# Moving the products of keys with values further back in a written-out order

## The chip, the cores and the metric

The kernel runs on one core of one Trainium2 chip. The metric is the device time of one execution in microseconds (us). Beside it a hardware profile of one execution is read: its span runs from the first to the last instruction.

## The reference

The inputs are queries, keys and values of 8 batches, 8 heads, 576 tokens and 64 features, and two weight matrices. The first block is an attention without a matrix of tokens by tokens; the second is a Fourier mix with a two-layer perceptron behind it.

```python
q_s = softmax of q over the features of a head
k_s = softmax of k over the tokens
kv  = np.einsum('bhsd,bhse->bhde', k_s, v)
x   = np.einsum('bhsd,bhde->bhse', q_s, kv)      # then heads side by side: (8, 576, 512)
u   = x + real(fft(fft(x, axis=1), axis=2))
un  = (u - mean(u)) / np.sqrt(var(u) + 1e-06)
out = u + np.maximum(un @ w_ch1, 0.0) @ w_ch2    # w_ch1: 512 x 2048, w_ch2: 2048 x 512
```

Everything is float32.

## The kernel before

The work goes batch by batch. A layer of the perceptron for one group of tokens runs on TensorE while the attention and the Fourier mix of the next group are threaded into it. The product with `w_ch1` is called *up* and the product with `w_ch2` *down*. Both use Strassen's scheme with seven products; in `up` a job of seven products is done four times (j = 0 to 3), and each uses two chunks of weights of 896 KB (`big<-w1s`), read from memory four chunks ahead. The products land in three banks, `ba`, `bb` and `bc`, in the order ba, bb, bc, bb, ba, bb, bc. Each product has two halves of four matmul instructions in the profile, and lines L1304, L1305, L1341, L1345 and L1346 bring the results from the banks, add and clip them on VectorE and ScalarE.

The order of all instructions is written by hand. Each piece of work is a *step* with a time; all steps of all groups are sorted by their time, and that order is what each engine gets. One unit of these times stands for 0.87 us. They are no waits: an engine runs its instructions in this order and waits only for data and buffers. The two halves of a product of `up` have one unit each.

`attention_timed(b, start, end)` gives the steps of the attention of batch b, which run during the `up` of the group before. `start` is 0 for b = 2 and 3 and -7 for b = 4 to 7. (Batches 0 and 1 have orders of their own.) In it:

- `keys(b)`: the maximum of the keys over the tokens (L695), exponentials (L699), and for each of four pairs of heads, r = 0 to 3: `turn` (L708, a transposition on VectorE of the keys), `times` (L715, the product of keys with values on TensorE, five matmul instructions of two passes), `scale` (L721 to L725, division by the sums on VectorE into the tile `kvr`).
- `values_to(b, h)`: four loads (L648) of one half of the values into the one tile `vt`. Half 0 serves r = 0 and 1, half 1 serves r = 2 and 3. Half 1 is loaded into the same tile, so it waits for the products r = 0 and 1.
- `keys_to(b)`: four loads (L638) of the keys of batch b into the one tile `kb`. The turned keys of r = 1 to 3 lie in that tile too, so the loads for the next batch wait for the product r = 3. `ahead(b)` places them, in the `up` of the group before.
- `own_exp`, `own_times_kv`: four query tiles (loads L743, maximum L756 on VectorE, subtraction L761 on GpSimd, transposition L764 on VectorE, exponentials `qT` L774 on ScalarE, product with `kvr` L790 on TensorE). For even b there is a shared tile of queries as well (turned by L912).
- `t_times_kv(b)`: the product of the shared tile with `kvr` (L1004).

All loads and most stores are issued by SyncE, one after the other; an issue that must wait holds back those behind it. Among them are the stores of results: rows as they are (L1611), and mirrored rows by way of memory, first out (L1618) and then from memory to memory (L1620).

Of the kernel before, what the change touches and what calls it, by code (L numbers as in the profile page):

```python
# [118 lines left out]
def at(t, script):  # L119
    return [(t + dt, step) for dt, step in script]  # L120
# [17 lines left out]
class _Block:  # L138
# [108 lines left out]
    def loads_first(self, fetch):  # L247
# [45 lines left out]
        def second(r):  # L293
# [4 lines left out]
            load(t[:, 4, :], self.v[1, S - P:, cols])  # L298

        order = [lambda: nc.gpsimd.memset(v[0:64, 4, :], 0.0), table, *(lambda r=r: keys(r) for r in range(NR)), lambda: queries(0),  # L300
                 lambda: values(0), lambda: queries(1), shared, lambda: values(2), shared_firsts, self.tables,
                 *(lambda r=r: second(r) for r in range(NR)), *(lambda i=i: fetch(i) for i in range(11))]
# [176 lines left out]
    def attention_timed(self, b, start, end):  # L479

        tail = [("t", b)] if b % 2 == 0 else []
        own = [("q", b, c, u) for c, u in ((0, 0), (0, 1), (1, 1), (1, 0))]
        places, shared = [6, 13.5, 21.5, 27.2], start + 12
        if tail:
            places = [8.5, 14, 21.5, 27.2]
        if start == 0:
            places, shared = [13.5, 20.5, 24, 27.2], 7
        steps = at(start, self.keys(b))
        for it in tail:
            steps += at(shared, self.q_exp(it)) + at(shared + 8, self.t_turn(it))  # L490
            steps += at(22.4 if start < 0 else 35, self.t_fold(it))
        for t, it in zip(places, own):
            steps += at(t, self.own_exp(it)) + at(t + 15, self.own_times_kv(it))
        loads = [(t - 7, t + 7.6, self.own_load(it)) for t, it in zip(places, own)]
        loads += [(shared - 13, shared + 8.4, self.t_load(it)) for it in tail]
        loads.sort(key=lambda s: s[0])
        free = [-99] * 3
        for i, (t, end, load) in enumerate(loads):
            if i > 1:
                steps += at(max(t, free[-3]), load)  # L500
            free.append(end)
        return steps + at((33 if start < 0 else 39) if tail else max(22, start + 26), self.t_times_kv(b))

    def ahead(self, b):


        steps = at(24 if b > 2 else 20, self.keys_to(b))
        steps += at(35 if b > 2 else 22.5, self.values_to(b, 0))
        q = [self.own_load(("q", b, 0, u)) for u in range(2)]
        if b % 2 == 0:  # L510
            q = [self.t_load(("t", b)), q[0]]
        return steps + at(46.5, q[0]) + at(50, q[1])
# [170 lines left out]

        return [(0, copies), (0.3 + 0.15 * (4 // by), least)]

    def keys(self, b):


        nc, V, kb = self.nc, self.nc.vector, self.kb
        box = {}  # L690

        def top(r):
            if r == 0:
                box["m"] = self.small.tile([P, 4 * NR], F32, tag="km16", name="km16", bufs=2)
            V.reduce_max(box["m"][:, 4 * r:4 * r + 4], kb[:, r], axis=AX.X, negate=True)  # L695

        def exp(g):
            k = kb[:, g // 4, g % 4]
            nc.scalar.activation(k, k, ACT.Exp, bias=box["m"][:, g:g + 1])  # L699

        def turn(r):
            if r == 0:
                t = self.work.tile([P, KT, HD], F32, tag="Z", name="Z", bufs=1)
                t = t[:].rearrange("p k n -> p (k n)")[:, 0:NC * P]
            else:
                t = kb[:, r - 1].rearrange("p g s -> p (g s)")
            to = box["k", r] = t.rearrange("p (c n) -> p c n", n=P)
            V.transpose(to.rearrange("p c (g s) -> p c g s", s=Q), kb[:, r].rearrange("p g (c s) -> p c g s", s=Q))  # L708

        def times(r):  # L710
            pk, k = self.acc((P, P + 1)), box.pop(("k", r))
            box[r] = pk
            a = (P + 1) * (r % 2)
            for c in range(NC):
                nc.tensor.matmul(pk, lhsT=k[:, c, :], rhs=self.vt[:, c, a:a + P + 1], start=c == 0, stop=c == NC - 1)  # L715

        def scale(r):
            pk = box.pop(r)
            rec = self.small.tile([P, 1], F32, tag="krec", name="krec", bufs=4)
            at = P * (r % 2)  # L720
            V.tensor_scalar(out=rec[:], in0=pk[:, at:at + 1], scalar1=ATT_EPS, scalar2=None, op0=ALU.add)  # L721
            V.reciprocal(rec[:], rec[:])
            for h in range(2):
                s, cols = slice(64 * h, 64 * h + 64), slice(64 * h + 1 - r % 2, 64 * h + 65 - r % 2)
                V.tensor_scalar(out=self.kvr[b % 2][s, r, s], in0=pk[s, cols], scalar1=rec[s, 0:1], scalar2=None, op0=ALU.mult)  # L725

        steps = [(0.9 * r, lambda r=r: top(r)) for r in range(NR)]
        steps += at(3.6, self.across(lambda: box["m"], 2, 4 * NR)) + at(4.5, self.across(lambda: box["m"], 1, 4 * NR))
        steps += [(6 + g / 2, lambda g=g: exp(g)) for g in range(4 * NR)]
        for r in range(NR):  # L730
            for dt, f in ((8.3, turn), (10.8, times), (12.5, scale)):
                steps.append((dt + 2 * r + 6 * (r > 1 and f != turn), lambda f=f, r=r: f(r)))
        steps += at(13.5, self.values_to(b, 1))
        return steps

    def own_load(self, it):
# [1038 lines left out]
```

## Time and profile before

| | us |
|---|---|
| median of 3 runs | 1054.22 |
| lowest, highest | 1052.79, 1058.33 |
| the profiled execution | 1057.53 |
| its span | 1055.8 |

In the rows of the timeline, the first number is the start in us from the span's start and the second the time to the end of the last of the instructions merged in the row; in brackets stands the idle time of the engine ahead of it and what ended it. A row of TensorE with x10 and line L715 is one product of keys with values. "PE" is TensorE, "DVE" VectorE, "ACT" ScalarE, "POOL" GpSimd and "SPq" the issuing of SyncE. Matmuls overlap by a little, so what one costs is read from one start to the next.

| | busy, us | share of the span |
|---|---|---|
| TensorE | 1037.7 | 98% |
| VectorE | 722.6 | 68% |
| ScalarE | 456.1 | 43% |
| GpSimd | 406.0 | 38% |

### The profile page before, as it was taken

To read this page: it belongs to the slowest core of one execution; us is meant where nothing else is said; L and a number is where in the kernel's file an instruction comes from. 1 tells how busy PE (TensorE), PEld (TensorE's weight loads), DVE (VectorE), ACT (ScalarE), POOL (GpSimd) and SP (SyncE) were. 2 spreads that over 40 slices of the span, in tenths; PEclk is the share of its full clock that TensorE was granted. 3 is DMA by queue.
4 is the path that set the end of the run, shared out by engine and by line. 5 is a ranking of instruction groups with operands and counts; after the bars stand their busy time and mean duration, and the time that the engine had idled before them with its cause. 6 is when DMAs were issued, how large, how long until landed. Compare 5 with 4: busy or idle time off the path is not lost.

```text
span 1055.8 us, 16768 instructions
## 1 busy us (share of the span) xinstructions
PE 1037.7 (98%) x6178; PEld 899.8 (85%) x6178; DVE 722.6 (68%) x1410; ACT 456.1 (43%) x1141; POOL 406.0 (38%) x350
## 2 busy tenths in 40 slices
PE   8999999899999999999999999999999999999998
PEld 7844555788888899889998999989998998999898
DVE  6898888665566876767765777688657644674563
ACT  5674433672248316751476236821682132131210
POOL 3164320257415645465545643474446450000000
PEclk9999999999999999999999999999999999999999
DMA  9787598586998666855677467757644664576464
GB/s 269 240 281 258 164 257 273 167 251 197 300 308 242 206 217 243 230 190 210 251 236 220 179 239 238 206 201 260 212 170 162 229 243 165 206 259 221 173 222 147
DMA packets 114313, 236.01 MB, mean 224 GB/s; under 512 B 23272, under 2 KB 78696, under 8 KB 103608
## 3 DMA queue, kind: packets, MB, share of 16 engines
q1 hardware_dynamic: 113864, 234.42, 67.7%
q8 instruction: 49, 0.80, 0.3%
q14 instruction: 32, 0.26, 0.1%
q10 hardware_dynamic: 288, 0.26, 0.1%
q0 software_dynamic: 80, 0.26, 0.1%
HBM read 199.79 MB, written 39.06 MB: 226 GB/s over the span
## 4 chain that ended last, share of the span: by engine, by line
PE 78%; DVE 5%; ACT 4%; DMA 3%; issue 1%; SPq 0%; POOL 0%; DVEq 0%; ACTq 0%
PE bb L1334 14%; PE bb L1461 10%; PE ba L1334 10%; PE bc L1334 9%; PE bc L1461 7%; PE ba L1461 7%; PE bb L1431 5%; PE acc L715 3%; ACT qT L774 2%; PE bb L1550 2%; PE acc L790 2%; PE acc L1087 1%; PE acc L1090 1%; DMA vt<-in_v_dram 1%; PE bc L1550 1%; PE ba L1550 1%
## 5 line engine op out<-in xcount | busy, mean ns | idle before, releaser
L1334 PE MATMUL bb<-unT,big 128*128 128x256 f32 x768 | 183.1, 381 | 0.1
L1334 PEld LDWEIGHTS bb<-unT,big 128*128 128x128 f32 x768 | 144.7, 191 | 19.9 <-DVE u L1304 1.0
L1346 ACT ACTIVATE big<-big 128x512 f32<-128x512 f32 x96 | 60.3, 629 | 170.8 <-DVE big L1345 169.9
L1334 PE MATMUL ba<-unT,big 128*128 128x256 f32 x512 | 124.0, 379 | 0.2 <-ACT big L1341 0.2
L774 ACT ACTIVATE qT<-q 32x128 f32<-32x128 f32 x384 | 117.9, 307 | 12.1 <-DVE q L764 7.1
L1334 PE MATMUL bc<-unT,big 128*128 128x256 f32 x512 | 121.8, 380 | 0.5 <-DVE big L1345 0.5
L1304 DVE TENSOR_TENSOR u<-bb,s 128x512 f32<-128x512 f32 x66 | 45.4, 687 | 94.5 <-PE bb L1334 79.5
L1334 PEld LDWEIGHTS bc<-unT,big 128*128 128x128 f32 x512 | 96.1, 190 | 14.2 <-DVE big L1345 1.8
L1334 PEld LDWEIGHTS ba<-unT,big 128*128 128x128 f32 x512 | 94.8, 190 | 12.6 <-ACT big L1341 0.6
L1461 PE MATMUL bb<-big 128*128 128x128 f32 x848 | 105.1, 275 | 0.3 <-DVE u L1468 0.3
L1461 PEld LDWEIGHTS bb<-big 128*128 128x128 f32 x848 | 99.6, 192 | 0.5 <-DVE u L1468 0.4
L1411 POOL TENSOR_TENSOR x<-x,big 128x512 f32<-128x512 f32 x45 | 57.7, 1296 | 63.5 <-DVE big L1468 31.2
L1461 PE MATMUL ba<-big 128*128 128x128 f32 x640 | 79.6, 275 | 0.0
L1461 PEld LDWEIGHTS ba<-big 128*128 128x128 f32 x640 | 76.3, 192 | 1.2
L1407 DVE TENSOR_TENSOR big<-big 128x512 f32<-128x512 f32 x98 | 75.3, 806 | 0.0
L761 POOL TENSOR_TENSOR q<-q,qm 128x512 f32<-128x512 f32 x24 | 25.8, 1073 | 116.1 <-DVE qm L756 73.0
L1210 POOL TENSOR_TENSOR unT<-unT 128x512 f32<-128x512 f32 x8 | 14.1, 1769 | 124.6 <-DVE unT L1210 124.6
L1468 DVE TENSOR_TENSOR u<-bb,s 128x256 f32<-128x256 f32 x40 | 16.8, 420 | 64.8 <-PE bb L1461 61.5
L1431 PE MATMUL bb<-big 128*128 128x256 f32 x256 | 58.7, 381 | 0.0
L384 POOL TENSOR_TENSOR big<-big 128x512 f32<-128x512 f32 x24 | 30.4, 1268 | 71.0 <-ACT big L1346 71.0
L1345 DVE TENSOR_TENSOR big<-bc,u 128x512 f32<-128x512 f32 x64 | 44.0, 687 | 18.6 <-PE bc L1334 17.8
L1431 PEld LDWEIGHTS bb<-big 128*128 128x128 f32 x256 | 48.2, 190 | 8.0 <-DVE big L1345 1.1
(279 smaller groups left out, 2032.2 us busy)
## 6 DMA issues: line engine op xcount, KB each, us to landing
big<-w2d SPq DMA_DIRECT2D x67, 1024.0 KB
big<-w1s SPq DMA_DIRECT2D x64, 896.0 KB
big<-w2s SPq DMA_DIRECT2D x16, 1024.0 KB
big<-in_w_dram SPq DMA_DIRECT2D x21, 512.0 KB
w2d<-big SPq DMA_DIRECT2D x42, 256.0 KB
kb<-in_kT_dram SPq DMA_DIRECT2D x24, 320.0 KB
q<-in_q_dram SPq DMA_DIRECT2D x28, 256.0 KB
vt<-in_v_dram SPq DMA_DIRECT2D x36, 160.0 KB
```

Of the source, the lines that this page charges most:

```text
L384: e1.tensor_tensor(out=to(4), in0=at(2), in1=at(3), op=ALU.add)
L715: nc.tensor.matmul(pk, lhsT=k[:, c, :], rhs=self.vt[:, c, a:a + P + 1], start=c == 0, stop=c == NC - 1)
L774: nc.scalar.activation(to[t, i * Q:i * Q + Q], one, ACT.Exp)
L1304: plus = lambda t: V.tensor_tensor(out=temp(t), in0=box["bb"][:], in1=box["s1"][:], op=ALU.add)
L1334: nc.tensor.matmul(bank()[:, i, :], lhsT=w[:, WA_AT[m], k * P:(k + 1) * P], rhs=self.unT[g][:, B_AT[m], k, :], start=first and i == 0 and ...
L1345: steps = [(0, lambda: V.tensor_tensor(out=hp(i), in0=bank()[:], in1=u()[:], op=ALU.add)), (0.8, lambda: nc.scalar.activation(hp(i), hp(i) ...
L1346: (0.8, lambda: nc.scalar.activation(hp(i), hp(i), ACT.Relu))]
L1407: e.tensor_tensor(out=to(o), in0=to(x), in1=to(y), op=op)
L1411: E.tensor_tensor(out=x, in0=x, in1=tile(m), op=ALU.add)
L1431: nc.tensor.matmul(box[name][:, i, :], lhsT=h[p][:, A_AT[m], i * P:(i + 1) * P], rhs=self.stream[n][:, p, :], start=p == 0 and (m != 1 or ...
L1461: nc.tensor.matmul(box[place[n]][:, i, :], lhsT=own(m)(A_AT[n])[:, f, :], rhs=w[:, r // 2, r % 2 * P:r % 2 * P + P], start=first and f == ...
L1550: nc.tensor.matmul(bank()[:, i, :], lhsT=h[p][:, A_AT[m], i * P:(i + 1) * P], rhs=w[:, p, :], start=first and i == 0 and p == 0, stop=p == ...
```

## The change

Only times of steps are changed. For all batches from 2 to 7, the products and scalings of r = 0 to 3 stand 1.5 units later, and so does the loading of the second half of the values. For b = 2 and 3 (start = 0), r = 2 and 3 stand another 2 units later, 3.5 in all. The loads of keys for b = 3 and 4 stand 3 units later (27 in place of 24), and the product of the shared tile's part for b = 3 follows (29 in place of 26; for b = 5 and 7 the larger of 22 and that is 22 in both). Nothing is computed differently, and no tile or buffer is added.

```diff
-        steps = at(start, self.keys(b))
+        steps = at(start, self.keys(b, start))
...
-        return steps + at((33 if start < 0 else 39) if tail else max(22, start + 26), self.t_times_kv(b))
+        return steps + at((33 if start < 0 else 39) if tail else max(22, start + 29), self.t_times_kv(b))
...
-        steps = at(24 if b > 2 else 20, self.keys_to(b))
+        steps = at(20 if b == 2 else 27 if b < 5 else 24, self.keys_to(b))
...
-    def keys(self, b):
+    def keys(self, b, start):
...
         for r in range(NR):
-            for dt, f in ((8.3, turn), (10.8, times), (12.5, scale)):
-                steps.append((dt + 2 * r + 6 * (r > 1 and f != turn), lambda f=f, r=r: f(r)))
-        steps += at(13.5, self.values_to(b, 1))
+            for dt, f in ((8.3, turn), (12.3, times), (14, scale)):
+                steps.append((dt + 2 * r + (6 + 2 * (start == 0)) * (r > 1 and f != turn), lambda f=f, r=r: f(r)))
+        steps += at(15, self.values_to(b, 1))
```

## The prediction

> **What bounds the kernel now.** I read the page first, then the waits of each engine, then the chain of waits and the timelines of the stretches in which TensorE stands still.
>
> ```profile
> span 1055.8 us, 16768 instructions
> PE 1037.7 (98%) x6178; PEld 899.8 (85%) x6178; DVE 722.6 (68%) x1410; ACT 456.1 (43%) x1141; POOL 406.0 (38%) x350
> ...
> PE acc L715 <- DMA vt<-in_v_dram: 2.8, 2, 2.7
> ```
>
> TensorE is busy for 98% of the span. The change adds and removes no arithmetic, so it can only win or lose stalls, and less than 20 us of stall exist. One of them belongs to the line that is moved: L715, the product of keys with values, waits 2.7 us for a load of values. The chain of waits shows how that arises in the group b = 2 (pieces: start, us, what).
>
> ```profile
> 192.07 1.13 PE acc L715 x10
> ...
> 195.03 8.41 DMA vt<-in_v_dram
> ...
> 203.53 2.39 PE acc L715 x10
> ```
>
> The second product (r = 1) frees the value tile at 193.20, SyncE issues the second half of the values, the third of those four loads, issued at 195.03, lands at 203.44, and only then can the third product (r = 2) start. TensorE's timeline gives the lateness (start, duration, instructions, idle time before).
>
> ```profile
> 188.20 1.03 PE L1334 MATMUL bb<-unT,big 128*128 128x256 f32 x4
> 189.06 1.28 PE L715 MATMUL acc<-vt,Z 128*128 128x129 f32 x10
> 190.18 1.03 PE L1334 MATMUL bb<-unT,big 128*128 128x256 f32 x4
> ...
> 191.91 1.28 PE L715 MATMUL acc<-vt,kb 128*128 128x129 f32 x10
> ...
> 195.61 0.60 PE L912 MATMUL tr<-ident,q 128*128 128x128 f32 x4
> 196.05 1.89 PE L1334 MATMUL bb<-unT,big 128*128 128x256 f32 x8
> 197.78 1.89 PE L1334 MATMUL bc<-unT,big 128*128 128x256 f32 x8
> 199.75 1.13 PE L1334 MATMUL bb<-unT,big 128*128 128x256 f32 x4
> 203.53 2.39 PE L715 MATMUL acc<-vt,kb 128*128 128x129 f32 x10 [2.65 <-DMA vt<-in_v_dram]
> ...
> 207.25 1.03 PE L1334 MATMUL ba<-unT,big 128*128 128x256 f32 x4
> ...
> 221.84 1.16 PE L790 MATMUL acc<-kvr,qT 128*128 128x130 f32 x8 [0.32 <-ACT qT L774]
> ```
>
> From start to start a half product of L1334 takes 0.86, a whole one 1.73, a product of keys with values 1.12, the turn of L912 0.44. After the row at 199.75 the row of 207.25 was due at 199.75 + 0.86 + 1.12 + 0.86 = 202.59. It is 4.66 late, 2 us more than the idle time. The windows say why (width, then busy times by engine, granted clock, DMA share and GB/s last):
>
> ```profile
> 200.60:203.50 2.90, 0.28 (x2) 0.00 (x0) 0.69 (x1) 2.15 (x7) 2.82 (x3) 1.00 1.06 262
> 203.65:207.06 3.41, 3.41 (x14) 3.14 (x15) 0.00 (x0) 0.00 (x0) 0.28 (x1) 0.50 0.26 105
> ```
>
> Right behind the stall the granted clock is 0.50 for 3.41 us, so about 1.7 us of work is lost again. The transfer queues are full (share 1.06) during the wait.
>
> **The change, part by part.** The order of instructions decides, so I take it from a comparison of the two programs. TensorE, VectorE, ScalarE and SyncE are reordered; GpSimd's order is the same.
>
> *b = 2, the stall.* The first two products move back by one whole product of L1334, the other two by two of them. r = 1 starts at 191.91 + 1.73 = 193.64 and ends at 194.76. Then come half a product, the turn, four whole products and a half before r = 2: 0.86 + 0.44 + 6.92 + 0.86 = 9.08, so r = 2 is due at 203.84 (before: 200.61). The loads cannot be issued before 194.8, 1.6 later than now. On SyncE, a query load (q) now stands ahead of all four of them instead of between the first and second:
>
> ```profile
> 192.10 0.32 SPq L455 DMA_DIRECT2D big<-w1s  x1
> 193.22 0.34 SPq L648 DMA_DIRECT2D vt<-in_v_dram  x1
> 193.60 0.44 SPq L743 DMA_DIRECT2D q<-in_q_dram  x1
> 194.08 2.08 SPq L648 DMA_DIRECT2D vt<-in_v_dram  x3
> ```
>
> The bytes ahead of the last values are the same: one weight chunk and one q. If the full queue sets the landing, it stays near 203.44, 0.4 before it is due, and the stall goes. If the issue sets it, it moves to about 205.1 and 1.3 us remain. I take the first, since the share is 1.06 up to the landing. Gain 4.66, bounds 2.9 (1.3 left, and a third of the clock loss) and 4.66. Also gained is 0.24 at 199.75 (due 199.51), where VectorE was busy with the results of r = 0 and 1.
>
> What is late next is the attention's L790. Its second run waits 0.32 before 221.84, for ScalarE, which went on without a gap that counts since 208.90:
>
> ```profile
> 208.90 0.63 ACT L1346 ACTIVATE big<-big 128x512 f32<-128x512 f32 x1 [6.08 <-DVE big L1345]
> ...
> 208.18 0.69 DVE L1345 TENSOR_TENSOR big<-bc,u 128x512 f32<-128x512 f32 x1
> ...
> 209.16 0.58 DVE L725 TENSOR_SCALAR kvr<-acc,krec 64x64 f32<-64x64 f32 x2
> ```
>
> ScalarE stood idle for 6.08 behind this same stall. In the new order the product on which this L1346 hangs runs ahead of r = 2, so ScalarE restarts before TensorE reaches r = 2; I count 0.3, bounds 0 and 0.32.
>
> *b = 2 and 3, the new wait.* The first L790 now follows the last product (r = 3) by two half products, 1.73, where three whole ones stood between. It needs the scaled result of r = 3, and on VectorE the L1345 of the half in between now comes first. From the end t of r = 3: t + 0.86 for the half, and 1.56 from the start of L1345 to the end of L725 (208.18 to 209.74), so t + 2.42; the last of L790's four matmuls arrives three quarters into its 1.0, at t + 1.73 + 0.75 = t + 2.48. Cost 0.2 in each group with the signals between engines, 0.4 in sum; bounds 0 and 2 each, if the query load whose maximum VectorE takes just before is late. Nothing else waits for that reordering: SyncE's next key loads come after r = 3 in both.
>
> *b = 3.*
>
> ```profile
> 313.28 1.28 PE L715 MATMUL acc<-vt,kb 128*128 128x129 f32 x10
> 320.44 1.03 PE L1334 MATMUL bb<-unT,big 128*128 128x256 f32 x4
> 321.65 1.35 PE L715 MATMUL acc<-vt,kb 128*128 128x129 f32 x10 [0.19 <-DMA vt<-in_v_dram]
> ...
> 339.50 1.16 PE L790 MATMUL acc<-kvr,qT 128*128 128x130 f32 x8 [0.48 <-ACT qT L774]
> ...
> 316.93 0.69 SPq L1620 DMA_DIRECT2D out_dram<-mirror  x1
> 317.67 3.51 SPq L1618 DMA_DIRECT2D mirror<-x  x1
> ...
> 315.93 5.59 DMA vt<-in_v_dram
> ```
>
> r = 2 is 0.35 late here (due 321.30), the second L790 0.48. In the new order r = 1 ends at 313.28 + 1.73 + 1.12 = 316.13 and r = 2 is due 8.64 later, at 324.77. But two stores that stood behind the values on SyncE now stand between the first load and the other three, and the issue behind the mirror copy L1620 lasts until 4.25 after the copy's. With the copy at about 316.6 the third load is issued near 321.3. With 5.59 to landing it comes at 326.9, 2.1 late; if it lands in 3, it is in time. The stores ahead are out of the way by then, so I take 0.3. Sum: 0.35 and half of 0.48, less 0.3: 0.3.
>
> *b = 4 to 7.* All four products move by one product of L1334, and so do their loads, behind stores that are ready.
>
> ```profile
>   DVE Z L708: 1.2, 4
> 418.44 1.30 PE acc L715 x10
> 421.46 1.11 PE acc L715 x10
> 430.11 1.50 PE acc L715 x10
> ```
>
> The first product waits for the turned keys (Z) in four groups; in b = 4 it takes 1.30 in the chain against 1.11 for the second, 0.19 lost. One product later the keys are long there: 4 x 0.19 = 0.8. The third one of b = 4 loses 0.39 at 430.11 to its loads; the distance from r = 1 to r = 2 stays, but the two stores now stand ahead of the loads and not among them: 0.3, bounds -0.5 and 0.39.
>
> *The keys of b = 3 and 4* are asked for later, three of the four loads now behind a weight chunk. That chunk gets earlier and is used by the last quarter of the layer; the keys are needed only in the next one. I cost this at nothing. The cover is that quarter's own time: transfers were done by 228, the quarter starts near 229.9, and each of its two chunks can be only about 2 us later before TensorE waits.
>
> ```profile
> 228.00:230.00 2.00, 2.00 (x13) 1.79 (x12) 0.69 (x2) 1.92 (x6) 0.00 (x0) 1.00 0.02 4
> 229.93 1.03 PE L1334 MATMUL ba<-unT,big 128*128 128x256 f32 x4
> ```
>
> **Sum.** 4.66 + 0.24 + 0.3 - 0.4 + 0.3 + 0.8 + 0.3 = 6.3 us. The profiled execution took 1057.53 (1055.8 of span and 1.7 around it), so it would take 1051.2. The median of the runs shown, 1054.22, is 3.3 lower; I lay the same difference on it: 1047.9.
>
> The Trainium skill, "TensorE: Matmul & The Clock Gate", Part 1, says that the clock is halved after at least one idle window of about 3.4 us. This trace has it halved after an idle time of 2.65, for 3.41. By the rule the stall alone would not have done it, and removing the stall would gain 1.7 less.
>
> **The rivals.**
> 1. *Landing follows issue* (b = 2): 1.3 us remain and part of the clock loss. For it speaks that all four loads now wait for r = 1 and cannot be queued earlier; against it the full queue. Gain 6.3 - 1.8 = 4.5: 1049.7. Chance 0.14.
> 2. *VectorE becomes the wait*: the load of the last query tile lands late, VectorE stands on its maximum, and L790 waits 1.5 us in b = 2 and 3. 3.0 in place of 0.4: gain 6.3 - 2.6 = 3.7: 1050.5. Chance 0.10.
> 3. *The clock drop is not the stall's*: it comes in any case, somewhere else. Against it speaks that it begins at 203.65, at the end of the longest wait in the middle of the kernel. Gain 6.3 - 1.7 = 4.6: 1049.6; by the skill's rule it would be this one. Chance 0.08.
> 4. *Slower: the mirror copy in b = 3.* The longest issue behind such a copy is in the row below: 5.87 us.
>
> ```profile
> 766.04 5.87 SPq L455 DMA_DIRECT2D big<-w1s  x1
> ```
>
> The copy's own issue ends at 317.3; with 5.87 behind it the third load is issued near 323.7, and with the 8.41 of b = 2 it lands at 332.1: 7.3 us of stall and 1.7 of clock against 6.6 of gain (6.3 without the 0.3 charged there). That ends 2.4 slower: 1056.6. It is slower from a landing at 329.7 on. Both extremes must meet, so 0.06.
> 5. *Nothing to win*: in other executions the stall of b = 2 may be shorter than in the slowest one profiled; the gain is then the small terms, 2 us: 1052.2. Chance 0.04.
>
> **How the numbers follow.** The forecast has 0.58 and its time, 1047.9. With all bounds in its favour (0.32 and no new wait in b = 2, 0.35 and 0.48 in b = 3) the gain is 7.2, and the fastest run shown, 1052.79, lies 1.4 under the median: 1045.6, rounded out to 1045.0. The upper end takes in rivals 1 to 3 and reaches half-way into the others: 1052.0. About 0.5%, 5.3 us, can be told from no change. Faster by more: most of the forecast (0.49) and the better parts of rivals 1 and 2 (0.06), 0.55. Slower by more needs rival 4 worse than priced, or an unseen wait: 0.05. The rest, 0.40, is within.
>
> **What would show it.** Right: no idle time over 1 us before L715 in b = 2, no stretch of clock 0.50 near 204, L790's second wait gone, the first products of b = 4 to 7 at 1.11. Wrong: a wait of L715 for values at b = 3 near 325, the first L790 of b = 2 or 3 waiting for VectorE over 0.5, or a wait of L1334 for weights near 225.

## The result and the profile after

| | us |
|---|---|
| before, median of 6 | 1054.43 (1052.79 to 1058.33) |
| after, median of 6 | 1049.08 (1047.82 to 1050.86) |
| ratio | 0.9946, 95% interval 0.9927 to 0.9965 |
| span of the profiled execution | 1049.1 (before 1055.8) |

The change saves 5.4 us by the medians, 0.5%; a second series, further down, gives a ratio of 0.9961 (0.9948 to 0.9974). Each ratio in this text is taken against the kernel before in the same series; its medians there were 1054.0 to 1055.7 us. The page and the waits of TensorE after:

```profile
span 1049.1 us, 16781 instructions
PE 1034.9 (99%) x6178; PEld 901.0 (86%) x6178; DVE 719.7 (69%) x1410; ACT 456.3 (43%) x1141; POOL 406.0 (39%) x350
...
PE ba L1334 <- DMA big<-w1s: 1.1, 1, 1.1
...
PE acc L790 <- DVE kvr L725: 0.4, 2, 0.2
```

The wait of L715 for values is gone from the list, and two new entries stand in it: L1334 for a weight chunk, and L790 for the result of VectorE. TensorE's timeline of b = 2:

```profile
194.39 1.28 PE L715 MATMUL acc<-vt,kb 128*128 128x129 f32 x10
...
204.65 1.28 PE L715 MATMUL acc<-vt,kb 128*128 128x129 f32 x10
...
207.49 1.28 PE L715 MATMUL acc<-vt,kb 128*128 128x129 f32 x10
...
210.33 0.83 PE L790 MATMUL acc<-kvr,qT 128*128 128x130 f32 x6
211.37 0.49 PE L790 MATMUL acc<-kvr,qT 128*128 128x130 f32 x2 [0.20 <-DVE kvr L725]
...
217.74 1.06 PE L790 MATMUL acc<-kvr,qT 128*128 128x130 f32 x8
```

The third product (204.65) starts without a wait; the second L790 (217.74) has lost its wait for ScalarE; the first one is held up before its last matmul. The clock, in the stretch that had 0.50 before (same columns as in the prediction):

```profile
200.60:203.50 2.90, 2.90 (x15) 2.56 (x14) 1.37 (x3) 2.61 (x9) 2.60 (x3) 1.00 0.80 321
203.65:207.06 3.41, 3.41 (x23) 3.13 (x21) 1.44 (x4) 3.22 (x9) 1.04 (x1) 1.00 0.02 5
```

The whole `up` of a group can be measured between two rows: from its first L1334 to the first matmul of the next stage. For b = 2 these are, before (first two rows) and after:

```profile
179.57 1.89 PE L1334 MATMUL ba<-unT,big 128*128 128x256 f32 x8
243.67 3.62 PE L1550 MATMUL ba<-big 128*128 128x256 f32 x16
```

```profile
180.32 1.89 PE L1334 MATMUL ba<-unT,big 128*128 128x256 f32 x8
238.61 3.62 PE L1550 MATMUL ba<-big 128*128 128x256 f32 x16
```

64.10 us become 58.29. The same difference, taken in all traces of this study, is the table that the rest is read from (us; "start" is where the first `up` begins, that is, how long all before it took):

| kernel | start | b=2 | b=3 | b=4 | b=5 | b=6 | b=7 |
|---|---|---|---|---|---|---|---|
| before | 179.57 | 64.10 | 59.34 | 58.53 | 57.48 | 58.34 | 57.49 |
| `again` (before once more) | 178.56 | 62.50 | 59.18 | 58.11 | 57.50 | 58.71 | 57.50 |
| after | 180.32 | 58.29 | 59.18 | 57.96 | 57.31 | 57.98 | 57.32 |
| `after_again` | 177.87 | 58.35 | 58.78 | 57.98 | 57.31 | 57.96 | 57.33 |
| `no_half` | 177.88 | 59.56 | 58.99 | 58.21 | 57.50 | 58.58 | 57.50 |
| `only_2` | 179.22 | 59.41 | 58.68 | 58.48 | 57.49 | 58.57 | 57.49 |
| `only_15` | 178.36 | 66.10 | 67.39 | 57.96 | 57.31 | 57.95 | 57.32 |
| `only_15b` | 178.90 | 58.86 | 59.77 | 57.96 | 57.32 | 57.97 | 57.32 |
| `only_late` | 179.48 | 61.49 | 59.50 | 57.97 | 57.31 | 57.95 | 57.31 |
| `only_loads` | 179.74 | 60.09 | 63.59 | 58.34 | 57.49 | 58.33 | 57.49 |
| `q_first_b2` | 178.70 | 61.50 | 59.44 | 58.12 | 57.49 | 58.31 | 57.49 |
| `chunks_first` | 178.88 | 58.29 | 58.04 | 57.96 | 57.31 | 57.97 | 57.31 |
| `queries_later` | 177.20 | 58.04 | 57.84 | 57.95 | 57.32 | 57.96 | 57.32 |
| `both_fixes` | 178.66 | 58.05 | 57.85 | 57.97 | 57.31 | 57.96 | 57.32 |

The stages between hardly change (57.23 us behind b = 2 in every trace). The start, which the change does not touch, varies by 3 us from one execution to the next, and so do the times. The change takes 5.81 us off b = 2 in this pair of profiles, 0.16 off b = 3 and 1.27 off b = 4 to 7.

### The profile page after: what moved, and what is told of

Same layout as the page of the kernel before. It is cut to its first block, busy times and chain, and to the rows that moved or that the text cites. A ratio compares the mean times of both kernels' runs of the same rounds, so it can differ in the third digit from the quotient of the medians.

```text
span 1049.1 us, 16781 instructions
## 1 busy us (share of the span) xinstructions
PE 1034.9 (99%) x6178; PEld 901.0 (86%) x6178; DVE 719.7 (69%) x1410; ACT 456.3 (43%) x1141; POOL 406.0 (39%) x350
## 4 chain that ended last, share of the span: by engine, by line
PE 81%; DVE 5%; DMA 3%; ACT 1%; issue 0%; POOL 0%; SPq 0%; DVEq 0%; ACTq 0%
PE bb L1334 15%; PE ba L1334 10%; PE bb L1461 10%; PE bc L1334 10%; PE bc L1461 7%; PE ba L1461 7%; PE bb L1431 5%; PE acc L715 2%; PE bb L1550 2%; PE acc L790 2%; DMA big<-w1s 2%; PE acc L1087 1%; PE acc L1090 1%; PE bc L1550 1%; PE ba L1550 1%; PE tr L1195 1%
## 5 line engine op out<-in xcount | busy, mean ns | idle before, releaser
L1334 PE MATMUL bb<-unT,big 128*128 128x256 f32 x768 | 182.0, 379 | 0.0
L1334 PEld LDWEIGHTS bb<-unT,big 128*128 128x128 f32 x768 | 144.3, 190 | 19.4 <-DVE u L1304 0.5
L1334 PE MATMUL ba<-unT,big 128*128 128x256 f32 x512 | 124.1, 379 | 1.1 <-DMA big<-w1s 1.1
L1334 PE MATMUL bc<-unT,big 128*128 128x256 f32 x512 | 121.7, 379 | 0.0
L1334 PEld LDWEIGHTS bc<-unT,big 128*128 128x128 f32 x512 | 96.1, 190 | 13.2 <-DVE big L1345 0.7
L1334 PEld LDWEIGHTS ba<-unT,big 128*128 128x128 f32 x512 | 94.5, 190 | 13.3 <-DMA big<-w1s 1.3
L1345 DVE TENSOR_TENSOR big<-bc,u 128x512 f32<-128x512 f32 x64 | 44.0, 687 | 19.6 <-PE bc L1334 18.6
```

What stands on the lines that cost most here:

```text
L1334: nc.tensor.matmul(bank()[:, i, :], lhsT=w[:, WA_AT[m], k * P:(k + 1) * P], rhs=self.unT[g][:, B_AT[m], k, :], start=first and i == 0 and ...
L1345: steps = [(0, lambda: V.tensor_tensor(out=hp(i), in0=bank()[:], in1=u()[:], op=ALU.add)), (0.8, lambda: nc.scalar.activation(hp(i), hp(i) ...
```

## The experiments

Where a diff of this section shows less than a line, the rest of the line is the same before and after.

**The same kernel before, once more (`again`).** No edit.

> The kernel before, unchanged, profiled once more. If the stall of b = 2 belongs to the order: TensorE again stands over 1.5 us before the third product of keys with values near 203, the third load of values lands 6 to 8.5 us after its issue, and the granted clock drops to 0.50 for 3.41 us right behind; span 1052 to 1056 us. If the wait was an accident of the one execution (transfers that ran slowly once): the loads land 4 to 5 us after their issue, as in the changed kernel (197.06 to about 200.9), and the wait is under 1 us, with no drop of the clock there; span 1049 to 1052 us.

The timeline of TensorE and the windows of the wait and of the time behind it:

```profile
202.54 1.40 PE L715 MATMUL acc<-vt,kb 128*128 128x129 f32 x10 [2.65 <-issue]
```

```profile
199.60:202.50 2.90, 0.29 (x2) 0.00 (x0) 0.69 (x1) 2.15 (x7) 2.82 (x3) 1.00 1.11 196
202.50:206.00 3.50, 3.46 (x23) 3.28 (x24) 1.12 (x2) 0.00 (x0) 0.45 (x1) 1.00 0.53 213
```

The wait is there again, 2.65 us, so it belongs to the order. (The row names "issue" as what ended it, but the third load lands at 202.45, just ahead of 202.54.) Its length belongs in part to the execution: `only_late`, further down, has the same order in b = 2 and waits 1.66 us there. The clock stays at 1.00 behind the wait, and b = 2 takes 62.50 and not 64.10. The time of this execution was 1055.15 us. The 1.6 us of the clock are no fixed part of the stall.

**The wait taken away at its cause (`no_half`).** It leaves the second half of the values of b = 2 out.

```diff
-        steps += at(13.5, self.values_to(b, 1))
+        if b != 2:
+            steps += at(13.5, self.values_to(b, 1))
```

> The kernel before without the four loads of the second half of the values of b = 2 (it leaves these values out: r = 2 and 3 of that batch use the first half's). It takes away the wait at its cause and moves nothing. If the stall with its clock drop is what the change removes in b = 2: 4.7 to 5.3 us under the kernel before in the profile (4.66 of lateness, 0.3 of ScalarE's wait), no clock of 0.50 near 204. If the clock drop is not the stall's: 3 us, and 3.41 us of clock 0.50 elsewhere. If the stall is short in most executions: 1 to 2.5 us in the rounds.

Ratio 0.9972 (0.9957 to 0.9986), 3.0 us, and 59.56 in b = 2: 2.94 under `again`. That is about what the stall costs without the drop of the clock: against `only_late`, where the wait was 1.66 us, it is 1.9, and the interval of the ratio reaches from 1.5 to 4.5. The 4.7 that stood first in the expectation was the profiled stall with its clock drop. With the four loads, this kernel also takes their bytes off the queues. The other waits of b = 2 stay, each as before:

```profile
215.60 1.16 PE L791 MATMUL acc<-kvr,qT 128*128 128x130 f32 x8 [0.32 <-ACT qT L775]
...
235.61 1.99 PE L1335 MATMUL bc<-unT,big 128*128 128x256 f32 x8 [0.50 <-DVE big L1346]
```

(A line more in this kernel: L791 is L790.) The whole change gets b = 2 to 58.29, 1.3 below that. So removing the stall and moving the products are two gains.

**One shift alone.** `only_15` has the 1.5 units without the other 2; `only_2` has the 2 units without the 1.5.

```diff
 only_15, against after
-    (6 + 2 * (start == 0)) * (r > 1 and f != turn)
+    6 * (r > 1 and f != turn)
-    at(20 if b == 2 else 27 if b < 5 else 24, self.keys_to(b))
+    at(24 if b > 2 else 20, self.keys_to(b))
 only_2, against after
-    for dt, f in ((8.3, turn), (12.3, times), (14, scale)):
+    for dt, f in ((8.3, turn), (10.8, times), (12.5, scale)):
-    steps += at(15, self.values_to(b, 1))
+    steps += at(13.5, self.values_to(b, 1))
```

> All products and the second half's loads 1.5 units later, without the other 2 units for r = 2 and 3 of b = 2 and 3 and without what follows them. In b = 2 the third product is due at 202.1 by the trace before, 7.4 us after r = 1 ends at 194.8. If the full queue sets the landing (203.44): 1.3 us of wait left, 3.5 us gained with the 1.1 of b = 4 to 7. If landing follows the issue by 8.4: 3 us left, 1.5 us gained, most of it in b = 4 to 7. If the loads land about 4 us after their issue, as in the changed kernel: no wait, 5 to 6 us gained, and the 2 units are not needed.

1065.44 us, ratio 1.0090 (1.0065 to 1.0114): slower. The shared tile's place is back at 26 too, but the cause is the line of the keys: with them at 24 and the product r = 3 at 24.3, the keys of the next batch are loaded into the tile ahead of that product (which thus reads a part of the wrong keys), and it has to wait for them. The third and fourth products of b = 2, and the clock from 207.94 on, while TensorE still waited:

```profile
200.94 1.28 PE L715 MATMUL acc<-vt,kb 128*128 128x129 f32 x10
208.95 2.52 PE L715 MATMUL acc<-vt,kb 128*128 128x129 f32 x10 [4.99 <-DMA kb<-in_kT_dram]
```

```profile
207.94:214.76 6.82, 5.81 (x19) 5.06 (x20) 1.47 (x5) 0.82 (x2) 0.00 (x0) 0.50 0.36 73
```

The question was not answered by the time, but two things were learnt. The later keys are a must of the change and no extra, and the third product ran at 200.94 without any wait for values.

> Only the 2 units for r = 2 and 3 of b = 2 and 3 (with the later keys and shared part that go with them); all else where it was. In b = 2 the third product is due at 202.3, 9.1 us after r = 1. If the landing stays at 203.44: 1.1 us of wait left, 3 us gained. If the loads land in 4 to 5 us: no wait, 4 to 5 us gained. The first products of b = 4 to 7 keep their 0.17 to 0.19 of loss each in both cases.

1052.53 us, ratio 0.9965 (0.9951 to 0.9978), 3.7 us gained. b = 2 falls to 59.41; the third product comes 0.18 after its due time, just behind the landing of the third load (202.20). b = 4 to 7 stay as they were.

**The shift of 1.5 with the keys left late (`only_15b`).** As `only_15`, but with the keys at 27.

> The 1.5 units for all products and loads without the other 2 units, this time with the later keys of b = 3 and 4, so that these loads stay behind the product r = 3. The trace of the first try has the values of b = 2 landed at 198.8, 3.7 us after their issue. If the loads land so soon because they are no longer queued right behind a weight chunk: no wait of r = 2 in b = 2 (due about 202), as much gained as by the whole change, 5 to 6 us. If the 2 units are needed: over 1 us of wait left at b = 2 or b = 3, and 1 to 3 us gained.

1050.80 us, ratio 0.9960 (0.9944 to 0.9975). In b = 2 no wait for values is left; the one for VectorE's L1345 stays. In b = 3 one for values is left:

```profile
201.48 1.28 PE L715 MATMUL acc<-vt,kb 128*128 128x129 f32 x10
...
235.93 1.99 PE L1334 MATMUL bc<-unT,big 128*128 128x256 f32 x8 [0.49 <-DVE big L1345]
...
318.48 1.35 PE L715 MATMUL acc<-vt,kb 128*128 128x129 f32 x10 [1.20 <-DMA vt<-in_v_dram]
```

So the 1.5 units alone clear the wait for values in b = 2, and the other 2 are needed in b = 3 (59.77 without them), where the mirror copy now stands among the loads. The wait for L1345 in b = 2 is in `only_2` too (0.49); it is gone only where both shifts are made, and b = 2 takes 58.86 here against 58.29.

**b = 4 to 7 alone (`only_late`).**

```diff
-    (10.8, times), (12.5, scale)
+    (10.8 + 1.5 * (start < 0), times), (12.5 + 1.5 * (start < 0), scale)
-    at(13.5, self.values_to(b, 1))
+    at(13.5 + 1.5 * (start < 0), self.values_to(b, 1))
```

> The 1.5 units for b = 4 to 7 alone; b = 2 and 3 as before. By the sum of the prediction 1.1 us gained (0.8 at the first products, 0.3 at the third), 0.9990 as ratio; the stall of b = 2 stays. If the shift there does more, for the loads that now stand behind the stores: 2 us or more.

Ratio 0.9986 (0.9972 to 1.0000), 1.5 us; 1.3 in the table's last four columns against the profile before. As priced, though the interval reaches from 0 to 3 us and the size rests on the table. The stall of b = 2 stayed, shorter:

```profile
202.46 1.39 PE L715 MATMUL acc<-vt,kb 128*128 128x129 f32 x10 [1.66 <-issue]
```

**The loads alone.** `only_loads` writes the second half's loads of b = 2 and 3 1.5 units later and moves no product; `q_first_b2` does it in b = 2 only.

```diff
 only_loads
-    at(13.5, self.values_to(b, 1))
+    at(13.5 + 1.5 * (start == 0), self.values_to(b, 1))
 q_first_b2
+    at(13.5 + 1.5 * (b == 2), self.values_to(b, 1))
```

> Only the second half's loads of b = 2 and 3 are written 1.5 units later; all products stay where they were. TensorE's order is that of before; on SyncE the query tile goes ahead of the values (b = 2), the mirror copy and a store between the first and the second load (b = 3). If it is the queue's bytes that set the landing (the theory of the prediction): the third load lands near 203.4 again, idle time 2.6 us, no gain. If being queued right behind the chunk is what makes it slow: landing near 200 to 201, idle time under 0.5 us, 2.5 to 3 us gained. At b = 3 1 to 3 us of new wait in both, since the mirror copy holds back three loads with no later product.

1059.01 us, ratio 1.0042 (1.0018 to 1.0067): slower. SyncE's order of b = 3, TensorE, and the clock behind it:

```profile
310.75 0.33 SPq L648 DMA_DIRECT2D vt<-in_v_dram  x1
311.18 0.81 SPq L1620 DMA_DIRECT2D out_dram<-mirror  x1
312.04 4.09 SPq L1618 DMA_DIRECT2D mirror<-x  x1
316.17 1.43 SPq L648 DMA_DIRECT2D vt<-in_v_dram  x3
```

```profile
320.40 2.37 PE L715 MATMUL acc<-vt,kb 128*128 128x129 f32 x10 [2.77 <-DMA vt<-in_v_dram]
```

```profile
320.55:323.96 3.41, 3.41 (x14) 3.14 (x15) 0.00 (x0) 0.00 (x0) 0.00 (x0) 0.50 0.73 273
```

The issue behind the mirror copy takes 4.09 us, the last three loads come 5 us after the first, and the stall is the one of b = 2 over again, clock and all. This is the course of rival 4, seen where no product moves away from it; that the copy is what makes the issue long is not shown by any run. In b = 2 the wait of the third product was down to 0.30.

> The kernel before, with one thing else: on SyncE the query tile of b = 2 goes ahead of the four loads of values in place of between the first and the second. All products stand where they were. In the kernel that did this for b = 2 and 3 the wait of the third product of b = 2 fell from 2.65 to 0.3 us. If the order of those loads is worth what it took off there: 2.3 us gained without a drop of the clock before, up to 4 where there was one, ratio 0.997 to 0.998. If the wait depends on the chance of one execution: no gain.

Ratio 1.0005 (0.9993 to 1.0018): nothing. The profile shows a wait of 1.70 us here, as long as the 1.66 of `only_late` with the loads where they were, so the 0.30 of `only_loads` was that execution's. Putting the query tile ahead of the loads is not what gains.

**The changed kernel again, and its two new waits.** `chunks_first` puts the keys of b = 3 and 4 behind both weight chunks, `queries_later` puts the first product of queries of b = 2 and 3 one half product later, `both_fixes` has both.

```diff
 chunks_first, against after
-    at(20 if b == 2 else 27 if b < 5 else 24, self.keys_to(b))
+    at(20 if b == 2 else 33 if b < 5 else 24, self.keys_to(b))
 queries_later, against after
-    at(t + 15, self.own_times_kv(it))
+    at(t + 15 + 1.4 * (start == 0 and t == 13.5), self.own_times_kv(it))
```

> The changed kernel once more, beside those of this call. If the wait of 1.24 us for a weight chunk at 343.7 in b = 3 belongs to the order (three key loads ahead of it): it comes again, over 0.5 us, and the loads of that stretch land late. If it was the chance of one execution: no wait there, and a span about 1.2 us shorter, near 1048. Ratio to before 0.993 to 0.996.

1049.42 us, ratio 0.9961 (0.9948 to 0.9974). The wait for the chunk came again, 0.69 us of idle time at 340.90; the chains of waits of the two executions of the changed kernel:

```profile
327.14 16.51 DMA big<-w1s
343.65 0.04 issue
343.69 1.13 PE ba L1334 x4
```

```profile
324.43 16.43 DMA big<-w1s
340.86 0.04 issue
340.90 1.13 PE ba L1334 x4
```

The second chunk takes 16.5 us from issue to landing, with three loads of keys ahead of it. Before, the four loads of keys and the first chunk were all ahead of it, and it took 10.3 us (10.0 in `again`); why the new order is slower is open.

> The changed kernel with the keys of b = 3 and 4 behind both weight chunks. If the chunk behind three key loads makes TensorE wait in most executions: 1.2 us faster than the changed kernel. If seldom: no difference (under 0.5). The waits of 0.47 before the first product of queries stay in both cases.

1048.38 us, ratio 0.9947 (0.9931 to 0.9963). b = 3 falls to 58.04, 0.7 to 1.1 under the two executions of the changed kernel; L790's waits stay.

> The changed kernel with the first product of queries of b = 2 and 3 one half product later. If the wait for the scaled result of r = 3 (0.47 us, twice) is a loss by itself: it goes, 0.9 us faster than the changed kernel. If it only moves to the next wait, for ScalarE's exponentials: no gain, and a wait before the second product of queries instead.

1048.62 us, ratio 0.9954 (0.9937 to 0.9971). L790's waits are gone; b = 2 falls by 0.25, about half of the 0.47; the other half comes back at the last product of b = 2, where L1345 was waited for before. This execution had no wait for the chunk, which landed 11.9 us after its issue, though its order on SyncE is that of the change: that wait comes in some executions and not in others. Without the edit of `chunks_first` two of three profiles have it, with the edit (there and in `both_fixes`) neither of two: too few to call the edit the cause. The three ratios of that series cannot be told apart by their intervals; the profiles' stages can.

> The change, with two edits more: in b = 2 and 3 the first product of queries one half product later, and the keys of b = 3 and 4 behind both weight chunks. It takes away the two waits that the changed kernel's trace shows: 0.47 us before that product, twice, and 1.24 us for a weight chunk at 343.7. If they are what is left: 0.9 us faster than the changed kernel from the first, and 1.2 from the second where that wait comes in each execution; 6 to 7.5 us under the kernel before. If the chunk's late landing is an accident of one execution: 0.9 alone, about 6 us.

1047.66 us (1046.15 to 1048.51), ratio 0.9924 (0.9906 to 0.9943): 8 us under the kernel before, and the lowest ratio and the lowest median of all that ran. It was not run in one series with the changed kernel, so how much of the difference to 0.9946 and 0.9961 is its own is known from the stages alone: 0.2 to 0.3 in b = 2 and 0.9 to 1.3 in b = 3.

## Why the prediction was right, step by step

The direction, the place and nearly the size were right: 1047.9 was forecast, 1049.08 measured. The terms of the sum as written add up to 6.2 and not 6.3 us. That the total came so near is in part luck: 1.7 too much for the clock stood against about 0.6 that was not foreseen in b = 2 and 0.2 to 0.4 in b = 4 to 7. The 4.6 us of rival 3 were as near to the 5.4 measured as the forecast was, and the second series gave 4.6.

- *The stall of b = 2.* Right: it went, and the theory that the order causes it holds (`again`, `no_half`). The term of 4.66 is the profiled execution's; in `again` the same idle time of 2.65 cost about 3 us, since the clock did not drop. The step that was mis-sized is laying the profiled difference on the median: 1.7 of it were clock, and `no_half` measures 3.0 for the stall as a mean of executions. Rival 3 was right that the drop is not tied to the stall, though not that it moves elsewhere: after has none between the opening and the end, and one in the opening (10.13 to 13.55), which the change does not touch and where before had none.
- *The landing.* Neither "the queue sets it" nor rival 1 came true. By the landing events of the traces the third load took 8.4 us from issue to landing before, 8.5 in `again`, 8.0 in `only_2`; issued 0.8 us later, counted from the start of `up`, it took 3.9 after, 3.5 in `after_again`, 4.0 in `only_15b`. The later load landed earlier: 20.2 us behind the start of `up` (200.49) instead of 23.9 (203.44). So the margin at the third product was 4 us and not 0.4, and the 2 units were not needed there for the values. The forecast that the stall goes was right, the landing that it rested on was not.
- *ScalarE's wait before the second L790 of b = 2* went, as priced (0.3); in b = 3 all of it went and not half. Not foreseen: the wait at 241.84, VectorE's L1345, 0.5 us idle and 0.65 from start to start, went as well. `no_half` kept both, so it is the new place of the products that removes them, not the end of the stall; the second took both shifts (`only_15b` and `only_2` keep it).
- *The new wait of L790.* Foreseen with its mechanism, 0.2 a time; measured 0.20 idle and 0.47 in all to the next start, of which 0.24 in b = 2 and 0.19 in b = 3 are won back when it is taken away (`both_fixes` against `chunks_first`). VectorE:

```profile
209.74 0.69 DVE L1345 TENSOR_TENSOR big<-bc,u 128x512 f32<-128x512 f32 x1
210.35 0.15 DVE L721 TENSOR_SCALAR krec<-acc 128x1 f32<-128x1 f32 x1
...
210.73 0.58 DVE L725 TENSOR_SCALAR kvr<-acc,krec 64x64 f32<-64x64 f32 x2
```

  L1345 starts 1.13 after the end of the product r = 3 (208.61), 0.27 later than the 0.86 that the working had; all else is as counted. Rival 2, the late query load, did not come.
- *b = 3.* 0.1 was forecast net of L790, 0.16 came in this pair, but by other parts: measured against `both_fixes` (57.85), 1.5 us of waits went and 1.3 came. The 0.3 for the mirror copy was not needed (no wait at 319.70); the issue behind it took 1.35 us, not 3.51. The cost of nothing for the keys was wrong in b = 3: the second chunk was asked for 2.4 us earlier in the group and landed 3.9 us later in it, 47.8 us behind the start of `up` in place of 43.9, and TensorE needs it at 46.6. The prediction had named that wait, but near 225, in b = 2.
- *b = 4 to 7.* 1.1 forecast, 1.27 in the profiles, 1.5 by `only_late`. The products after (chain of waits, b = 4) take 1.11 to 1.12 each:

```profile
414.88 1.12 PE acc L715 x10
417.72 1.11 PE acc L715 x10
426.39 1.11 PE acc L715 x10
```

## What to carry to other kernels

In an order written by hand, a load that reuses a tile is paid by the distance from the last use to the next one: measure how long the load takes there, and place the products so far apart, with all that its queue puts in between. Further executions of the same order tell which part of a stall is fixed: lay only that part on the median. When a stall goes, look at the loads that were just in time behind it; here a chunk that had been 2 us early became the next wait.

## What the runs showed of the hardware

Idle time of TensorE and the clock: 1.20 (`only_15b`), 1.66 (`only_late`) and 1.70 us (`q_first_b2`) were followed by no drop; 2.65 was, in one of two executions; 2.77 was (`only_loads`); 4.99 was, for 6.82 us (`only_15`). Each drop, but for those at the program's end, lasted 3.41 us or twice that. The changes of the clock lie whole steps of 3.413 us apart in the records (before, 58 of them from 5.67 to 203.65). Counted in these steps, the whole idle time of 2.65 fell into one step before (200.23 to 203.65), and 1.79 of the 2.65 into one in `again`. Behind the opening, a drop followed each step with 2.24 us of idle time or more (`before`, `only_loads`, `only_15`) and none with 1.79 or less at full clock; in the opening, 1.56 (after) and 1.82 (`only_loads`) were followed by one. The Trainium skill, "TensorE: Matmul & The Clock Gate", Part 1, says that the window of 3413 ns runs on its own and does not start with the kernel; that the same wait drops the clock in one execution and not in the next agrees with it. Its threshold of about 3.4 us of idle does not: 2.65 was enough.

Of the same four loads of values, the third took 7.9 to 8.5 us to land where the first was issued 1.1 us behind a weight chunk (four executions; 8.1 and 6.9 with the query load ahead, `q_first_b2` and `only_loads`), and 3.3 to 4.7 where it was issued 4 us behind it (seven executions). The chunk itself took 8.0 us before and 7.1 in `again`, 5.2 after and 4.9 in `after_again`, but 4.6 in `only_loads`. Why is open: the packets' order on the transfer engines was not separated by any run.
